# Two-layer decode step: a group's softmax issued ahead of the next group's first K, and the last group's softmax in a place of its own

## The chip, the cores and the metric

The kernel runs on one core of one Trainium2 chip. The metric is the device time of one execution in microseconds (us); a kernel is timed several times and the median is given. Beside the times there is a profile of one execution, taken by the hardware. PE is TensorE's matmul pipe (PEld its weight loads), DVE is VectorE, ACT is ScalarE, POOL is GpSimd, and SP is SyncE, which here does nothing but issue the transfers (DMAs) in a fixed order. SBUF is the on-chip memory, PSUM the place where matmuls leave their results.

## The reference

One token of width 640 passes twice through an attention block and a mixer with an MLP, with the same weights and the same caches both times:

```python
x = x + A(layernorm(x))     # layer 0 in the code, the first layer
x = x + B(layernorm(x))
x = x + A(layernorm(x))     # layer 1 in the code, the second layer
x = x + B(layernorm(x))
```

A has 32 heads of 192 elements, each with its own K and V: `q = x @ wq`, scores of q with the last W = 4096 rows of K, divided by sqrt(192), a softmax `p` over these 4096, `o = p @ V`, and `o @ wo`. B is a layer norm, `gelu(x @ w1)`, a shift along the sequence, `@ w2`, a residual sum, and `gelu(layernorm(x1) @ w3) @ w4`. With one token the four shifts bring only zeros in, so that the path through w1 and w2 gives nothing; the kernel loads w3 and w4 alone. All is bf16. K and V of one head are 1.5 MB each, and they do not fit on the chip: both layers read most of them from HBM, 216 MB in all.

## The kernel before, in words

**Heads and groups.** Heads go in 8 groups of 4 (`QH`), in layer 0 from the last heads to the first (`GROUPS[0].reverse()`): 28 to 31, 24 to 27, and so on, then 8 to 11 (`gi` = 5), 4 to 7 (`gi` = 6) and 0 to 3 (`gi` = 7). Layer 1 goes from the first group to the last. The main loop, from L797, does two things in one turn `gi`: it multiplies the softmax of group `gi` with that group's V, and it makes the scores of group `gi + 1` from that group's K.

**Steps.** Their names in the code and their main lines are:

- `T(h, half)`: two of the four quarters of a head's K are transposed by DVE (L422).
- `S(h, half, ...)`: the scores of these quarters, 12 matmuls into `ST_ps` (L501).
- `softmax_steps` (L521) gives seven steps for a group. `part_max`: maximum per partition (L529, DVE). `turn_max`: its transpose on PE (`pmT_ps`, L535). `full_max`: the maxima per head, written out wide (L544 to L548, DVE). `spread_max`: broadcast by a matmul (`nb_ps`, L557), then the exponentials on ACT (L565). `turn_p`: P's transpose on DVE (L570) and its sums (L572, L573). `swap`: P brought into the order in which V lies (`PT_ps`, L582, on PE; L585 on ACT), and the total `l_ps` (L588). `recip`: its reciprocal (L595, L597, DVE).
- `pv(layer, h, hq, PT, first, mid)`: P V of one head, 16 matmuls into `O_ps` (L629). After every second head DVE transposes `O_ps` into `o_sb` (L638), and `o_fold` (L640) sums up from there by matmuls (`oT_ps`, L649) and scales on ACT (L652). `mid` is a step that is issued in the middle of the 16 matmuls.
- `qproj_steps` (four steps: project, spread, repeat, block): the query of the group after next (L452, L466, L473, L483).
- `out_row` with its sums (L678, L688), `turn_row` (L700), `out_proj` (L660) and `add_y`: the group before goes through wo, and into the residual sum.

In a turn these are interleaved: the first K quarters of the next group come ahead of `part_max`, its other transposes and scores between the further softmax steps, and so on. The two last turns are special: in the last but one (`hurry`), the remaining K heads are transposed and scored after the second P V, and the last group's softmax is made in the same turn around the fourth P V. The last turn (`final`) only multiplies with V.

**Places.** K, V, wo, w3 and w4 live in 11 cells (`cells`) of 1.5 MB. A written plan (`home`, L118) says which cell a load goes to. The loads are issued by SP in one fixed order (`stream`, L283). A load waits until its cell has been read by whatever used it, and all loads behind it in the order wait with it. Around the change the order is, with cells in brackets: K 4 and 5 [0, 1], V 8 and 9 [2, 3], K 6 [4], V 10 [7], K 7 [9], V 11 [8], wo of group 2 [0], K 0 [2], V 4 [7, and a last piece into the small buffer `kx`], K 1 [4], V 5 [10], K 2 [8], K 3 [7], V 6 [0], V 7 [10], V 0 [8], wo, V 1 [0], wo, V 2 [8], V 3 [7], w3 [0], w4 [8]. Cell 10 holds the transposed K of the heads that aren't kept until head 7 has been scored. K of heads 0 to 6 stays on chip, transposed, for layer 1. Parts of w3 and w4 are kept for both layers in `wx_sb`; until they are loaded, rows of that buffer serve as scratch (`row_space`, L397), and in layer 1 `kx` does.

**Order on the engines.** On PE, DVE, ACT and SP each engine executes its instructions in the order in which the code issues them (`manual_schedule`); a wait holds all that stands behind it on the same engine. Small PSUM results share two places (`psm`, `bufs=2`). In the softmax, the wide maxima and P lie in the bytes of `o_sb` (`o_bytes`, L519), so a softmax and an O that is being folded can't be there at once:

```python
    o_sb = big.tile([P, 2, NA, 32], F32, name="o_sb")
    o_bytes = o_sb[:].rearrange("p e c i -> p (e c i)").bitcast(BF16)
```

Of the kernel before, what the change touches and what calls it, by code (L numbers as in the profile page):

```python
# [8 lines left out]
F32 = mybir.dt.float32  # L9
# [7 lines left out]
P = 128  # L17
# [17 lines left out]
def kernel(  # L35
# [482 lines left out]
    o_sb = big.tile([P, 2, NA, 32], F32, name="o_sb")  # L518
    o_bytes = o_sb[:].rearrange("p e c i -> p (e c i)").bitcast(BF16)  # L519

    def softmax_steps(n, ST_ps, sc):  # L521
        held = {}

        def by_head(t):
            return t.rearrange("p (x e) -> p e x", e=2)

        def part_max():
            pm = big.tile([P, 2], F32, name="pm")
            nc.vector.tensor_reduce(out=pm[:], in_=by_head(ST_ps), op=ALU.max, axis=AX.X)  # L529
            held["pm"] = pm  # L530

        def turn_max():
            pmT_ps = psm.tile([1, 2 * (P + HB)], F32, tag="psm")
            for e in range(2):
                nc.tensor.transpose(pmT_ps[0:1, e * P:(e + 1) * P], held["pm"][:, e:e + 1], ident[:, :])  # L535
            held["pmT"] = pmT_ps

        def full_max():
            ngm = big.tile([1, 2, 2], F32, name="ngm")
            wide = o_bytes[0:1, SW:3 * SW].bitcast(F32)  # L540
            own = held["pmT"][0:1, :].rearrange("o (e y) -> o e y", e=2)[:, :, 0:P]
            for e in range(2):
                rows = wide[:, e * P:(e + 1) * P].rearrange("o (q e x) -> o q e x", q=NT, e=2)
                nc.vector.memset(rows[:, :, 1 - e], NEVER)  # L544
                nc.vector.tensor_reduce(  # L545
                    out=ngm[0:1, e], in_=own[:, e].rearrange("o (q x) -> o q x", q=NT)[:, :, 0:HB].rearrange(
                        "o q (r z) -> o r q z", r=2), op=ALU.max, axis=AX.XY, negate=True)
                nc.vector.tensor_scalar(  # L548
                    out=rows[:, :, e].rearrange("o q (r z) -> o q r z", r=2),
                    in0=ngm[0:1, e].unsqueeze(1).unsqueeze(3).broadcast_to([1, NT, 2, 2 * NM]),  # L550
                    scalar1=sc[0:1, 0:1], scalar2=None, op0=ALU.mult)
            held["w"] = wide

        def spread_max():
            nb_ps = psm.tile([P, 2], F32, tag="psm")
            for e in range(2):
                nc.tensor.matmul(nb_ps[:, e:e + 1], lhsT=held["w"][:, e * P:(e + 1) * P],  # L557
                                 rhs=one[0:1, 0:1], start=True, stop=True)
            nb_sb = big.tile([P, 2], F32, name="nb_sb")
            nc.scalar.copy(nb_sb[:], nb_ps[:])  # L560
            Pr = o_bytes[:, 0:SW]
            held["PrT"] = o_bytes[:, SW:2 * SW]
            lpart = big.tile([P, 2], F32, name="lpart")
            for e in range(2):
                nc.scalar.activation(out=by_head(Pr)[:, e], in_=by_head(ST_ps)[:, e], func=ACTF.Exp,  # L565
                                     bias=nb_sb[:, e:e + 1], scale=sc[:, 0:1], accum_out=lpart[:, e:e + 1])
            held["Pr"], held["l"] = Pr, lpart

        def turn_p():
            nc.vector.transpose(held["PrT"], held["Pr"])  # L570
            lh = big.tile([P, QH], F32, name="lh")
            nc.vector.tensor_add(held["l"][:, 0:1], held["l"][:, 0:1], held["l"][:, 1:2])  # L572
            nc.vector.tensor_scalar(out=lh[:], in0=hm[:], scalar1=held["l"][:, 0:1], scalar2=None, op0=ALU.mult)  # L573
            held["lh"] = lh

        def swap():
            ng = NGK // NT
            PT_ps = psm.tile([P, 2 * n, NJ4, NGK], F32, tag="psm")
            src = held["PrT"].rearrange("p (g j i) -> p i j g", g=ng, j=NJ4)
            for m in range(NM):  # L580
                for q in range(NT):
                    nc.tensor.matmul(PT_ps[32 * m:32 * (m + 1), :, :, ng * q:ng * (q + 1)], lhsT=Eq[:, q, :],  # L582
                                     rhs=src[:, m:QW:NM], start=True, stop=True)
            PT = big.tile([P, n, NJ4 * NGK, 2], BF16, name="PT")
            nc.scalar.copy(PT[:].rearrange("p h c e -> p e h c"),  # L585
                           PT_ps[:].rearrange("p (e h) j g -> p e h (j g)", e=2))
            l_ps = psm.tile([P, QH], F32, tag="psm")
            nc.tensor.matmul(l_ps[:], lhsT=ones, rhs=held["lh"][:], start=True, stop=True)  # L588
            held["lps"] = l_ps
            return PT  # L590

        def recip():
            lq = big.tile([P, QH], F32, name="lq")
            rl = sm.tile([P, 1], F32, name="rl")
            nc.vector.scalar_tensor_tensor(out=lq[:], in0=held["lps"][:], scalar=1.0, in1=blkm[:],  # L595
                                           op0=ALU.mult, op1=ALU.mult, accum_out=rl[:, 0:1])
            nc.vector.reciprocal(rl[:], rl[:])  # L597
            return rl

        return part_max, turn_max, full_max, spread_max, turn_p, swap, recip  # L600
# [103 lines left out]
    def attention(layer, x_cur, rs_cur, x_new, z_new, rs_new, ss_new):  # L704
# [13 lines left out]
        def T(h, half):  # L718
            for q in (2 * half, 2 * half + 1):
                if (h, q) not in Th:  # L720
                    Th[h, q] = transpose_quart(layer, h, q)
# [75 lines left out]
        for gi, cur in enumerate(groups):  # L797
            nxt = list(enumerate(groups[gi + 1])) if gi + 1 < len(groups) else []
            ST_n = None
            if nxt:  # L800
# [24 lines left out]
                else:  # L825
                    if gi == 0:
                        for step in q1:
                            step()
                    h0 = nxt[0][1]
                    T(h0, 0)  # L830
                    part_max()
                    T(h0, 1)
                    S(h0, 0, ST_n, 0)
                    turn_max()
                    full_max()
                    S(h0, 1, ST_n, 0)
                    spread_max()
                    h1 = nxt[1][1]
                    q = None
                    if gi + 2 < len(groups):  # L840
                        q = qproj_steps(groups[gi + 2][0] // QH, xc, row=q_row if gi in rows else None)
# [2 lines left out]
                    in_row = gi - 1 in rows  # L844
                    if pending is not None:
                        y_ps = out_row(layer, *pending, acc, gi - 1 == rows[0]) if in_row else out_proj(layer, pending)
                    turn_p()
                    T(h1, 0)
                    if q:
                        q[1]()  # L850
                        q[2]()
                    if in_row:
                        y_ps()
                        if gi - 1 == rows[-1]:
                            add_y(turn_row(acc), 1 if layer == 1 and gi + 2 == len(groups) else 2)
                        pending = None
                    if pending is not None:
                        add_y(y_ps, 1 if layer == 1 and gi + 2 == len(groups) else 2)
                        pending = None
                    PT = swap()  # L860
                    T(h1, 1)
                    if q:
                        q[3]()
                    rl = recip()
                    nxt.pop(0)
            else:
                PT, rl = early
# [6 lines left out]
                order = [order[n] for n in (VC, VP, 0, 1)]  # L874
            for n, (hq, h) in enumerate(order):
                first = n % 2 == 0
                pv(layer, h, hq, PT, first, fold)
                if final:
                    if layer == 0 and hq == 0:
                        add_y(out_proj(layer, pending), 1)  # L880
                    if hq == 1:
                        center_y()
                    fold = None
                    if not first:
                        def fold(h=h):
                            o_fold(h, oT, rl)

                    continue
                if hurry and hq == 1:
                    (q2, h2), (q3, h3) = nxt  # L890
                    for half in range(2):
                        T(h2, half)
                        S(h2, half, ST_n, q2)
                    T(h3, 0)
                    S(h3, 0, ST_n, q3)
                    T(h3, 1)
                elif hurry and hq == 2:
                    S(h3, 1, ST_n, q3)
                    steps = softmax_steps(len(cur), ST_n, sc)
                    steps[0]()  # L900
                    steps[1]()
                elif nxt and not (hurry and hq == 3):
                    q2, h2 = nxt.pop(0)
                    for half in range(2):
                        T(h2, half)
                        S(h2, half, ST_n, q2)
                if not first:
                    o_fold(h, oT, rl, len(groups) - 4 > gi >= 2 * layer)
                if hurry and hq == 3:
                    for step in steps[2:5]:  # L910
                        step()
                    early = steps[5](), steps[6]()
            if final:
                fold()
# [151 lines left out]
```

## Time and profile before

| | |
|---|---|
| median of 3 runs | 522.64 us (521.62 to 523.77) |
| the profiled execution's own time | 522.96 us |
| its span (first to last instruction) | 521.2 us |
| busy: PE, DVE, ACT | 60%, 55%, 9% of the span |
| mean granted TensorE clock | 0.709 of full speed |
| read from HBM | 216.47 MB, 415 GB/s over the span |
| DMA engines, share of the span | 98.1% for SP's queue |

How to read it: the page cuts the span into 40 equal slices of 13 us and gives for each the busy tenths of every engine, the granted clock, the DMA engines' share and GB/s. The chain that ended last is the work followed back from the last instruction, at each step to what released it. A row of the timeline is start, duration, engine, line, operation, destination and source, count, and in brackets the idle time ahead of it on its engine with what ended it. "SPq" is SP's queue, where a row is the issue of a transfer and not its landing.

### The profile page before, as it was taken

How to read it: one execution, taken by the hardware profiler on the slowest of the kernel's cores; microseconds unless marked ns; L12 is line 12 of the kernel's file. 1: busy time of each engine (PE TensorE's matmuls, PEld its weight loads, DVE VectorE, ACT ScalarE, POOL GpSimd, SP SyncE). 2: the span in 40 equal slices, each digit the busy share in tenths (PEclk: the TensorE clock that was granted, in tenths of full speed). 3: DMA queues.
4: the chain of work that ended last, by engine and by line, in shares of the span. 5: the costliest groups of instructions: out<-in, count | busy, mean ns of one | idle time of the engine just before them, and what ended most of it. 6: DMA issues, size and time to landing. Idle time of an engine off the chain costs nothing.

```text
span 521.2 us, 9518 instructions
## 1 busy us (share of the span) xinstructions
PE 314.6 (60%) x4132; PEld 195.0 (37%) x4132; DVE 285.3 (55%) x642; ACT 48.8 (9%) x173; POOL 4.0 (1%) x16
## 2 busy tenths in 40 slices
PE   1045866656473664767655876757485674645776
PEld 0023434324242332545333644433243342333445
DVE  2057576657564674476623366657446674646723
ACT  1000101010010100101011111010010100100011
POOL 2000000000000000000000000000000000000000
PEclk9999568756778566566765687686656677875667
DMA  8999999999999999979999999999999999999995
GB/s 349 436 434 433 418 441 428 429 435 424 440 429 429 429 431 426 427 309 397 429 423 415 371 419 430 433 435 427 428 437 428 430 433 430 425 436 426 423 409 226
DMA packets 17613, 217.07 MB, mean 417 GB/s; under 512 B 1828, under 2 KB 2340, under 8 KB 7972
## 3 DMA queue, kind: packets, MB, share of 16 engines
q1 hardware_dynamic: 17572, 216.48, 98.1%
q8 instruction: 32, 0.52, 0.4%
q14 instruction: 9, 0.07, 0.0%
HBM read 216.47 MB, written 0.00 MB: 415 GB/s over the span
## 4 chain that ended last, share of the span: by engine, by line
DMA 45%; PE 24%; DVE 23%; ACT 4%; issue 3%; SPq 1%; DVEq 0%; ACTq 0%
DMA cells<-in_A_k_cache_dram 40%; DVE cells L422 16%; PE ST_ps L501 10%; PE O_ps L629 4%; DMA cells<-in_A_v_cache_dram 4%; ACT o_sb L565 3%; PE nb_ps L557 2%; DMA cells<-in_B_w_dram 2%; PE pmT_ps L535 1%; PE PT_ps L582 1%; DVE o_sb L570 1%; DVE o_sb L638 1%; DVE pm L529 1%; PE y_ps L700 1%; PE y_ps L1011 1%
## 5 line engine op out<-in xcount | busy, mean ns | idle before, releaser
L422 DVE STREAM_TRANSPOSE cells<-cells 128x768 uint32<-128x768 uint32 x228 | 203.7, 946 | 49.2 <-DMA cells<-in_A_k_cache_dram 49.0
L501 PE MATMUL ST_ps<-cells,Qblk 128*32 128x256 bf16 x1536 | 150.0, 373 | 118.0 <-DVE pm L529 65.7
L501 PEld LDWEIGHTS <-Qblk 128*32 128x32 bf16 x1536 | 89.6, 123 | 174.6 <-issue 154.1
L629 PE MATMUL O_ps<-cells,PT 128*4 128x384 bf16 x1018 | 93.5, 450 | 10.4 <-DMA cells<-in_A_v_cache_dram 10.0
L638 DVE STREAM_TRANSPOSE o_sb<-O_ps 128x384 f32<-128x384 f32 x32 | 18.7, 583 | 78.2 <-PE O_ps L629 78.2
L629 PEld LDWEIGHTS <-PT 128*4 128x4 bf16 x1024 | 43.5, 103 | 26.7 <-issue 16.3
L652 ACT ACTIVATE oT<-oT_ps,rl 64x6 bf16<-64x6 f32 x32 | 8.4, 262 | 228.8 <-PE oT_ps L649 128.3
L570 DVE STREAM_TRANSPOSE o_sb<-o_sb 128x256 bf16<-128x256 bf16 x16 | 7.1, 445 | 37.7 <-ACT o_sb L565 37.7
L582 PE MATMUL PT_ps<-o_sb,Eq 128*32 128x64 bf16 x256 | 11.0, 293 | 10.7 <-DVE lpart L572 5.5
L560 ACT COPY nb_sb<-nb_ps 128x2 f32<-128x2 f32 x16 | 2.6, 161 | 134.8 <-PE nb_ps L557 134.8
L582 PEld LDWEIGHTS <-Eq 128*32 128x32 bf16 x256 | 7.4, 112 | 20.5 <-issue 20.4
L565 ACT ACTIVATE o_sb<-ST_ps,nb_sb,sc 128x128 bf16<-128x128 f32 x32 | 15.0, 491 | 0.5
L452 PE MATMUL qT_ps<-xc,wq_sb 128*128 128x1 bf16 x210 | 7.1, 165 | 13.0 <-DMA wq_sb<-in_A_wq_dram 12.1
L557 PEld LDWEIGHTS nb_ps<-one,o_sb 1*128 1x128 f32 x64 | 12.2, 261 | 6.9 <-issue 4.9
L557 PE MATMUL nb_ps<-one,o_sb 1*128 1x1 f32 x64 | 13.6, 309 | 1.5 <-DVE ngm L545 1.5
L678 PE MATMUL yr_ps<-cells,oT 128*1 128x320 bf16 x108 | 14.5, 432 | 0.0
L441 PE MATMUL qr_ps<-wq_sb,xc 128*1 128x384 bf16 x90 | 13.5, 452 | 0.0
L588 PE MATMUL l_ps<-lh,one 128*128 128x4 f32 x32 | 8.3, 329 | 6.8 <-ACT PT L585 6.8
L466 DVE TENSOR_TENSOR Xq<-qT_ps,maskq 128x24 bf16<-128x24 f32 (+1 forms) x18 | 2.8, 155 | 16.9 <-PE qT_ps L452 16.9
L452 PEld LDWEIGHTS <-wq_sb 128*128 128x128 bf16 x210 | 6.7, 101 | 14.0 <-DMA wq_sb<-in_A_wq_dram 13.2
L649 PE MATMUL oT_ps<-o_sb,Lq 128*32 128x6 f32 x160 | 7.2, 190 | 7.7 <-DVE o_sb L638 7.7
L585 ACT CAST PT<-PT_ps 128x256 bf16<-128x256 f32 x16 | 7.1, 445 | 47.8 <-PE PT_ps L582 47.8
(146 smaller groups left out, 193.9 us busy)
## 6 DMA issues: line engine op xcount, KB each, us to landing
cells<-in_A_k_cache_dram SPq DMA_DIRECT2D x23, 3072.0 KB, 20.5
cells<-in_A_v_cache_dram SPq DMA_DIRECT2D x22, 3072.0 KB, 22.6
cells<-in_A_v_cache_dram SPq DMA_DIRECT2D x12, 1536.0 KB, 12.5
cells<-in_A_k_cache_dram SPq DMA_DIRECT2D x11, 1536.0 KB, 13.7
cells<-in_A_wo_dram SPq DMA_DIRECT2D x13, 960.0 KB, 28.3
wq_sb<-in_A_wq_dram SPq DMA_DIRECT2D x5, 1536.0 KB, 13.7
cells<-in_A_v_cache_dram SPq DMA_DIRECT2D x6, 768.0 KB, 15.2
cells<-in_A_v_cache_dram SPq DMA_DIRECT2D x2, 1248.0 KB, 11.4
```

Source lines behind the costliest of these rows:

```text
L422: nc.vector.transpose(Tu, Ku[:, :, q * NY:(q + 1) * NY])
L441: nc.tensor.matmul(qr_ps[32 * i:32 * i + 1, :], lhsT=xc[:, kc:kc + 1], rhs=wq_sb[:, kc, t0 * P + i * N:t0 * P + (i + 1) * N], start=(kc == ...
L452: nc.tensor.matmul(qT_ps[:, tl:tl + 1], lhsT=wq_sb[:, kc, t * P:(t + 1) * P], rhs=xc[:, kc:kc + 1], start=(kc == 0), stop=(kc == ND - 1))
L501: nc.tensor.matmul(ST_ps[r:r + QW, :].rearrange("p (g i) -> p g i", g=ng), lhsT=Q[:, n, :], rhs=T4[:, :, f, :, t], start=(hq == 0 and n == ...
L557: nc.tensor.matmul(nb_ps[:, e:e + 1], lhsT=held["w"][:, e * P:(e + 1) * P], rhs=one[0:1, 0:1], start=True, stop=True)
L565: nc.scalar.activation(out=by_head(Pr)[:, e], in_=by_head(ST_ps)[:, e], func=ACTF.Exp, bias=nb_sb[:, e:e + 1], scale=sc[:, 0:1], accum_out ...
L570: nc.vector.transpose(held["PrT"], held["Pr"])
L582: nc.tensor.matmul(PT_ps[32 * m:32 * (m + 1), :, :, ng * q:ng * (q + 1)], lhsT=Eq[:, q, :], rhs=src[:, m:QW:NM], start=True, stop=True)
L629: nc.tensor.matmul(O_ps[r:r + 4, :], lhsT=PT[:, hq, 2 * i:2 * i + 2].rearrange("p c e -> p (c e)"), rhs=v_pair(V, h, 2 * i * Dh, 2 * Dh), ...
L638: nc.vector.transpose(o_sb[:], O_ps.rearrange("p (e a c) -> p e c a", e=2, c=NA))
L652: nc.scalar.activation(oT[r, :], oT_ps[r, :], ACTF.Copy, scale=rl[r, 0:1])
L678: nc.tensor.matmul(yr_ps[32 * i:32 * i + 1, :], lhsT=oT[:, k:k + 1], rhs=wo_t[:, k * D + i * N:k * D + (i + 1) * N], start=(k == 0), stop= ...
```

## The change

It has three parts.

First, in layer 0, in the turns `gi` = 5 and 6 (`ahead`), the first four softmax steps of group `gi` are issued before any K of the next group, and `turn_p` before the first transpose of K; the query's steps, the row sums, `swap` and `recip` follow that first transpose, then scores and the other transposes. Both heads `h0` and `h1` are transposed before the first P V. All other turns keep their order.

Second, in the last but one turn of both layers (`hurry`), the scores of the last quarter of K and the maximum (`steps[0]`) are issued ahead of the third head's P V, the next three steps right behind it, and `turn_p` (`steps[4]`) in the middle of the fourth.

Third, that last group's softmax gets a place of its own (`room`): a part of `wx_sb` in layer 0, where w4 is loaded later, and `kx` in layer 1, in place of the bytes of `o_sb`.

```diff
-    def softmax_steps(n, ST_ps, sc):
+    def softmax_steps(n, ST_ps, sc, room=None):
+        room = o_bytes if room is None else room
...
-            wide = o_bytes[0:1, SW:3 * SW].bitcast(F32)
+            wide = room[0:1, SW:3 * SW].bitcast(F32)
...
-            Pr = o_bytes[:, 0:SW]
-            held["PrT"] = o_bytes[:, SW:2 * SW]
+            Pr = room[:, 0:SW]
+            held["PrT"] = room[:, SW:2 * SW]
...
-                    h0 = nxt[0][1]
-                    T(h0, 0)
-                    part_max()
-                    T(h0, 1)
-                    S(h0, 0, ST_n, 0)
-                    turn_max()
-                    full_max()
-                    S(h0, 1, ST_n, 0)
-                    spread_max()
-                    h1 = nxt[1][1]
+                    h0, h1 = nxt[0][1], nxt[1][1]
+                    ahead = layer == 0 and gi + 3 >= len(groups)
+                    if ahead:
+                        for step in (part_max, turn_max, full_max, spread_max):
+                            step()
+                    else:
...
+                    if ahead:
+                        turn_p()
+                        T(h0, 0)
+                        if q:
+                            q[1]()
+                        if in_row:
+                            y_ps()
+                        else:
+                            add_y(y_ps, kind)
+                        PT, rl = swap(), recip()
+                        S(h0, 0, ST_n, 0)
+                        T(h0, 1)
+                        if q:
+                            q[2]()
+                            q[3]()
+                        if in_row and gi - 1 == rows[-1]:
+                            add_y(turn_row(acc), kind)
+                        S(h0, 1, ST_n, 0)
+                        T(h1, 0)
+                        T(h1, 1)
+                    else:
...
-                pv(layer, h, hq, PT, first, fold)
+                if hurry and hq == 2:
+                    S(h3, 1, ST_n, q3)
+                    steps = softmax_steps(len(cur), ST_n, sc, (wx_sb[:, 16 * P:22 * P], kx)[layer])
+                    steps[0]()
+                pv(layer, h, hq, PT, first, steps[4] if hurry and hq == 3 else fold)
...
                 elif hurry and hq == 2:
-                    S(h3, 1, ST_n, q3)
-                    steps = softmax_steps(len(cur), ST_n, sc)
-                    steps[0]()
-                    steps[1]()
+                    for step in steps[1:4]:
+                        step()
...
                 if hurry and hq == 3:
-                    for step in steps[2:5]:
-                        step()
                     early = steps[5](), steps[6]()
```

More of the change, by code (lines that the diff above doesn't have):

```diff
@@ L828, in attention @@
                             step()
-                    h0 = nxt[0][1]
-                    T(h0, 0)
-                    part_max()
-                    T(h0, 1)
-                    S(h0, 0, ST_n, 0)
-                    turn_max()
-                    full_max()
-                    S(h0, 1, ST_n, 0)
-                    spread_max()
-                    h1 = nxt[1][1]
+                    h0, h1 = nxt[0][1], nxt[1][1]
[5 more added lines that the diff above has]
+                        T(h0, 0)
+                        part_max()
+                        T(h0, 1)
+                        S(h0, 0, ST_n, 0)
+                        turn_max()
+                        full_max()
+                        S(h0, 1, ST_n, 0)
+                        spread_max()
                     q = None
@@ L846, in attention @@
                         y_ps = out_row(layer, *pending, acc, gi - 1 == rows[0]) if in_row else out_proj(layer, pending)
[L847 to L864, printed above, removed]
+                    kind = 1 if layer == 1 and gi + 2 == len(groups) else 2
+                    if ahead:
+                        turn_p()
+                        T(h0, 0)
+                        if q:
[5 more added lines that the diff above has]
+                        PT, rl = swap(), recip()
+                        S(h0, 0, ST_n, 0)
+                        T(h0, 1)
+                        if q:
[3 more added lines that the diff above has]
+                            add_y(turn_row(acc), kind)
+                        S(h0, 1, ST_n, 0)
+                        T(h1, 0)
+                        T(h1, 1)
+                    else:
+                        turn_p()
+                        T(h1, 0)
+                        if q:
+                            q[1]()
+                            q[2]()
+                        if in_row:
+                            y_ps()
+                            if gi - 1 == rows[-1]:
+                                add_y(turn_row(acc), kind)
+                        elif pending is not None:
+                            add_y(y_ps, kind)
+                        PT = swap()
+                        T(h1, 1)
+                        if q:
+                            q[3]()
+                        rl = recip()
@@ L865, in attention @@
+                    pending = None
                     nxt.pop(0)
```

## The prediction

> **What bounds the kernel now.** I read the page's slices and chain first, then the busy time of stretches, then the issues of SP's queue, then the instructions between them. The page:
>
> ```profile
> DMA  8999999999999999979999999999999999999995
> GB/s 349 436 434 433 418 441 428 429 435 424 440 429 429 429 431 426 427 309 397 429 423 415 371 419 430 433 435 427 428 437 428 430 433 430 425 436 426 423 409 226
> ...
> DMA cells<-in_A_k_cache_dram 40%; DVE cells L422 16%; PE ST_ps L501 10%; PE O_ps L629 4%; DMA cells<-in_A_v_cache_dram 4%; ACT o_sb L565 3%; PE nb_ps L557 2%; DMA cells<-in_B_w_dram 2%; PE pmT_ps L535 1%; PE PT_ps L582 1%; DVE o_sb L570 1%; DVE o_sb L638 1%; DVE pm L529 1%; PE y_ps L700 1%; PE y_ps L1011 1%
> ```
>
> The DMA engines move some 430 GB/s in nearly every slice, and K's transfers are 40% of the chain that ends last: a stream of bytes sets the time. Beside start and end, three slices fall short: the 18th (309 GB/s) with the 19th (397), and the 23rd (371), the border of the two layers. What can be won is what the stream loses there. The first dip, by stretches: the stretch, its length, busy us of PE, PEld, DVE, ACT and POOL with their instructions, the granted TensorE clock, the DMA engines' busy share, GB/s:
>
> ```profile
> 206.00:209.00 3.00, 3.00 (x25) 1.39 (x21) 2.19 (x8) 0.00 (x0) 0.00 (x0) 0.50 0.91 389
> 209.00:212.00 3.00, 3.00 (x44) 2.30 (x46) 0.75 (x4) 1.15 (x5) 0.00 (x0) 0.50 1.04 442
> 224.00:227.00 3.00, 1.57 (x13) 0.90 (x13) 3.00 (x5) 0.00 (x0) 0.00 (x0) 0.50 1.01 430
> 227.00:228.00 1.00, 0.72 (x13) 0.39 (x12) 1.00 (x2) 0.00 (x0) 0.00 (x0) 0.50 0.81 344
> 228.00:231.00 3.00, 2.92 (x48) 2.07 (x46) 2.92 (x4) 0.26 (x1) 0.00 (x0) 0.50 0.25 107
> 231.00:233.00 2.00, 1.67 (x27) 1.10 (x26) 0.29 (x1) 0.00 (x0) 0.00 (x0) 0.89 0.78 205
> 233.00:242.00 9.00, 5.54 (x84) 3.66 (x84) 5.70 (x15) 1.74 (x7) 0.00 (x0) 0.79 1.00 375
> 242.00:290.00 48.00, 29.82 (x444) 18.72 (x444) 21.49 (x64) 4.73 (x20) 0.00 (x0) 0.61 1.02 422
> 302.00:514.00 212.00, 134.59 (x1753) 83.75 (x1752) 121.35 (x263) 20.80 (x75) 0.71 (x2) 0.70 1.01 428
> 498.00:501.00 3.00, 1.44 (x26) 0.63 (x27) 1.46 (x7) 0.26 (x1) 0.00 (x0) 1.00 1.01 412
> ```
>
> A full queue gives 422 to 428 GB/s; I count with 425. Against that, 227 to 228 lacks 81 KB, 228 to 231 lacks 3 x 318 = 954 and 231 to 233 2 x 220 = 440: 1475 KB, or 1475 / 425 = 3.5 us of stream lost. 233 to 242, where the engines are busy again but slow, lacks 9 x 50 = 450 KB, another 1.1 us. Why the queue ran dry stands among SP's issues (start, duration) and in what SP waited for:
>
> ```profile
> 198.47 0.60 SPq L164 DMA_DIRECT2D cells<-in_A_k_cache_dram  x1
> 212.55 0.54 SPq L178 DMA_DIRECT2D cells<-in_A_v_cache_dram  x1
> ...
> 220.48 0.53 SPq L164 DMA_DIRECT2D cells<-in_A_k_cache_dram  x1
> 229.96 0.54 SPq L178 DMA_DIRECT2D cells<-in_A_v_cache_dram  x1
> ```
> ```profile
> SPq L178 <- PE O_ps L629: 8.9, 1, 8.9
> ```
>
> The load at 229.96 is V of head 4. Its place is cell 7, which V of head 10 holds until the product P V of that head (L629) has read it, and SP, which issues in order, stood 8.9 us for it. So the length of the work from K of heads 4 and 5 (landed at 203.39) to P V of head 10 (229.96) decides: 26.6 us. The instructions of that stretch:
>
> ```profile
> 197.90 0.58 DVE L638 STREAM_TRANSPOSE o_sb<-O_ps 128x384 f32<-128x384 f32 x1 [3.01 <-PE O_ps L629]
> ...
> 198.53 0.30 PE L649 MATMUL oT_ps<-o_sb,Lq 128*32 128x6 f32 x8 [0.68 <-DVE o_sb L638]
> ...
> 203.39 1.84 DVE L422 STREAM_TRANSPOSE cells<-cells 128x768 uint32<-128x768 uint32 x2 [4.91 <-DMA cells<-in_A_k_cache_dram]
> 205.15 0.39 DVE L529 TENSOR_REDUCE pm<-ST_ps 128x2 f32<-128x256 f32 x1
> ...
> 205.59 1.47 PE L501 MATMUL ST_ps<-cells,Qblk 128*32 128x256 bf16 x12 [6.75 <-DVE pm L529]
> ...
> 213.69 0.96 DVE L688 TENSOR_TENSOR wx_sb<-wx_sb,yr_ps 1x320 f32<-1x320 f32 x2
> ...
> 214.71 2.26 PE L700 MATMUL y_ps<-ident,wx_sb 33*128 33x1 f32 x12 [0.71 <-DVE wx_sb L688]
> ...
> 218.47 0.59 PE L588 MATMUL l_ps<-lh,one 128*128 128x4 f32 x2 [0.59 <-ACT PT L585]
> 218.99 1.45 PE L629 MATMUL O_ps<-cells,PT 128*4 128x384 bf16 x16
> 219.30 0.16 DVE L597 RECIPROCAL rl<-rl 128x1 f32<-128x1 f32 x1
> ...
> 223.45 0.58 DVE L638 STREAM_TRANSPOSE o_sb<-O_ps 128x384 f32<-128x384 f32 x1 [3.99 <-PE O_ps L629]
> ...
> 236.77 0.59 PE L535 MATMUL pmT_ps<-ident,pm 128*1 128x128 f32 x2
> ...
> 240.43 0.45 DVE L570 STREAM_TRANSPOSE o_sb<-o_sb 128x256 bf16<-128x256 bf16 x1 [2.12 <-ACT o_sb L565]
> ```
>
> DVE idles 4.91 us ahead of 203.39, for K. The scores of heads 8 to 11 are complete by then, but their softmax starts only at 205.15, interleaved with the new K, so P V of head 8 begins at 218.99.
>
> **Part 1: the softmax ahead (layer 0, groups of heads 8 to 11 and 4 to 7).** No operation is added; they move. DVE is free from 197.90 + 0.58 = 198.5. The maximum is 0.39; from its turn (236.77) to P's transpose (240.43) took 3.66, and the transpose is 0.45, with two small sums behind it at the 0.16 of the row of 219.30: 198.5 + 0.4 + 3.7 + 0.8 = 203.4. That fits the idle 4.91 us almost exactly, so K's transpose starts at 203.4 as before. Then, in the new order:
>
> - K of head 4, first half, 1.84: 205.2. Behind it on DVE stand a step of the query (0.16) and the row sums, 0.96: 206.4. The turn of P on PE runs beside them; it waits only for the query's step, which gives a PSUM place back.
> - The row total l_ps 0.59 and the reciprocal, 2 x 0.16: 207.4. Second half of K, 1.84: 209.3; the first half's scores (1.47) lie beside it.
> - The turned row y_ps, 2.26 on PE, from about 209.0, with its sum: 211.5. Then the second scores, 1.47: 212.8. Both halves of head 5's transposes, 2 x 1.84 behind that sum: 215.2.
> - P V of head 8, 1.45 beside the transposes: 214.3. Head 5's scores need the last transpose: 215.2 + 1.47 = 216.7. P V of head 9: 216.7 + 1.45 = 218.1.
>
> O's transpose (L638) thus starts at about 218.1, against 223.45: 5.3 us earlier. From there the order is the old one, so V of head 4 is issued near 229.96 - 5.3 = 224.7; the K ahead of it follows P V of head 8, near 214.3 instead of 220.48. V of head 8 should not hold this up: its 3 MB were queued right behind K of heads 4 and 5, so they land near 203.4 + 3.146 MB / 425 GB/s = 210.8 (an estimate from these rows).
>
> When must the issue come? The engines were full until 227, and the issue of 229.96 brought bytes only in the row of 231: about 1.1 us. So 226 keeps them full; 224.7 leaves 1.3 us. The next loads in SP's order wait for transposes and P V that move with it.
>
> For the next group, heads 4 to 7, the same softmax (0.4 + 3.7 + 0.8 = 4.9 us) stands between O's transpose, 5.3 us earlier, and the transposes of K of head 0. These start no later than now, with the softmax already behind them, so the loads that this group's P V releases come early enough for a stream that is ahead by 3.5. The **gain is 3.5 us** if the queue no longer dries up; I take that, because it is the part with idle engines. The bounds: 2.9 by the busy share alone (0.19 + 3 x 0.75 + 2 x 0.22 = 2.9), and 4.5 if the slow 233 to 242 was all restart too. I leave that 1.1 us out, because V of head 4 is cut in two pieces in the new order too.
>
> **Part 2: the last maximum ahead, P in its own place.** In layer 0 it is covered by transfers: the chain there runs through landings (K 10.81 and B_w 8.53, below). In layer 1 nothing covers it:
>
> ```profile
> 231.24 10.81 DMA cells<-in_A_k_cache_dram
> ...
> 279.44 8.53 DMA cells<-in_B_w_dram
> ...
> 450.04 19.11 DMA cells<-in_A_k_cache_dram
> 469.24 1.84 DVE cells L422 x2
> ```
> ```profile
> 497.90 0.42 DVE L529 TENSOR_REDUCE pm<-ST_ps 128x2 f32<-128x256 f32 x1 [2.38 <-PE ST_ps L501]
> ...
> 498.69 0.82 PE L629 MATMUL O_ps<-cells,PT 128*4 128x384 bf16 x16
> ...
> 503.74 0.70 PE L582 MATMUL PT_ps<-o_sb,Eq 128*32 128x64 bf16 x16 [1.80 <-DVE lpart L572]
> ...
> 504.98 1.45 PE L629 MATMUL O_ps<-cells,PT 128*4 128x384 bf16 x16
> ```
>
> From 469.24 to the end the chain is work alone. Before: maximum 497.90, turn of P 503.74, last group's P V 504.98. After: the scores no longer wait for the third P V, so the maximum comes some 0.85 earlier, 497.05. Its turn now stands behind that P V on PE (497.0 + 1.45): 498.5. 3.66 later, 502.1, P's transpose, with its sums to 502.9; O's transpose is queued behind it on DVE, 0.58: 503.5; the fold's matmuls, 0.30 and a start just behind it (198.53 after 198.48): 503.9; there the turn of P may start. So 0.2 later than now, where the fourth P V had no wait ahead of it. With the third P V at 0.82 in place of 1.45 it is 0.5 earlier; with 0.4 more lost in the 3.66 to a slower clock (its pmT alone is 0.59), 0.6 later than now. I take **0**, with -0.5 to +0.6. The fresh place costs no copy; it only frees this softmax from waiting until O has been read.
>
> A rule bears on those bounds. The Trainium skill (TensorE: Matmul & The Clock Gate, Part 1) has TensorE's clock halved by default and released after some 3.4 us of sustained work; the new wait inside the fourth P V's queue would by that rule cost the 0.4 and so the 0.6, and 522.64 would become 519.7 rather than 519.1. The trace does not follow the rule here: 1.00 was granted in 498 to 501 with PE busy under half the time, and 0.50 through 206 to 212 with PE busy throughout.
>
> **Sum.** The profiled execution took 522.96 us for a span of 521.2; with 3.5 less it is 519.5. The median of the three runs is 0.32 below that execution: 522.64 - 3.5 = **519.1 us**. A stretch gained before 242 is kept if the queue stays full (422 and 428 GB/s in the two long rows) and the border's dip, which starts from a landing (279.44, 8.53), shifts with it.
>
> **Rivals.** (B) The queue still dries up, for less time. For it: only 1.3 us of margin, and a softmax that fits its gap to 0.1 us. Against it: the rows are those of the half-speed clock already. Each us beyond the margin costs a us; with 2 to 3 us too late about 1.3 us is won: 521.3. (C) The transfer is hidden anyway: what the first layer wins is given back at the border (371 GB/s in the 23rd slice would sink further), or the tail is the real bound. For it: the tail from 469.24 has no transfer in its chain. Against it: that chain starts at a landing. It gives 522.6, with the tail's -0.5 to +0.6. (D) Slower: on PE the scores of head 4 now stand behind the turn of P and l_ps, which stand behind DVE's rows, which stand behind K's transpose. If these waits follow one another rather than overlap, the stretch from 203.39 to head 10 grows. It decides once it is longer than the present 26.6 us (my sum: 21.3); at 29.6 the queue is dry for 3 us more, and the time is 525.6. Against it: it takes 5.3 us of error in ten short rows.
>
> **How the numbers follow.** A measurement of this kernel tells about 0.5%, 2.6 us, from no change. Forecast 0.60 (517.5 to 519.9), B 0.17, C 0.12, D 0.11. The low end is 522.64 - 4.5 - 0.5 = 517.6; the high end reaches over B to C's middle, 522.6. Left out are D, half of C and a little below: under 0.2. Faster by over 0.5%: the forecast but for its slow edge, 0.58; within: 0.02 + 0.17 + 0.12 = 0.31; slower: 0.11.
>
> **What would show it.** In the changed profile: the softmax between 198.5 and 203.4; P V of head 8 near 213 to 214 rather than 218.99; V of head 4 issued before 226; no stretch under 0.9 DMA share between 224 and 242; the border's landing (287.97 now) and the last K's (469.15 now) both some 3.5 us earlier; the last group's first P V as far behind the last K as now (504.98 - 469.2 = 35.8 us, to within 0.6). I am wrong if V of head 4 is issued after 227, or if the last K lands earlier and the end doesn't follow.

## The result and the profile after

The changed kernel takes 519.02 us (median of 6, 518.16 to 519.44) against 523.20 us of the kernel before, measured beside it: a ratio of 0.992, 95% interval 0.9901 to 0.9939. The profiled execution took 518.16 us with a span of 516.4, against 522.96 and 521.2.

The stretches of the profile after, in the same columns as before (last three: granted clock, DMA share, GB/s):

```profile
224.00:227.00 3.00, 2.16 (x35) 1.16 (x28) 1.39 (x3) 0.00 (x0) 0.00 (x0) 1.00 1.01 423
227.00:228.00 1.00, 0.46 (x10) 0.33 (x10) 0.76 (x3) 0.20 (x1) 0.00 (x0) 1.00 0.99 419
228.00:231.00 3.00, 1.86 (x36) 1.59 (x35) 0.90 (x6) 1.21 (x6) 0.00 (x0) 0.74 0.99 413
231.00:233.00 2.00, 0.99 (x18) 0.68 (x17) 1.97 (x5) 0.44 (x1) 0.00 (x0) 0.50 1.01 426
233.00:242.00 9.00, 6.59 (x55) 3.68 (x56) 5.83 (x11) 0.00 (x0) 0.00 (x0) 0.50 1.02 432
```

The dry stretch is gone. From 227 to 242 the rows now carry 419 + 3 x 413 + 2 x 426 + 9 x 432 = 6398 KB; before they carried 344 + 3 x 107 + 2 x 205 + 9 x 375 = 4450. At 425 GB/s the difference is 4.6 us, and the span is 4.8 us shorter. The slow 233 to 242 went with the rest. V of head 4 still comes in two pieces, and the rows from 227 to 233, in which most of their packets move, hold 413 to 426 GB/s. The packet records of the two traces show the difference: the 128 packets of the larger piece, 9984 bytes each, all took 375 ns in the full queue, where they had averaged 499 behind the gap.

The instructions that made the room (timeline after; lines behind L521 are one higher than before, later ones more):

```profile
197.87 0.39 DVE L530 TENSOR_REDUCE pm<-ST_ps 128x2 f32<-128x256 f32 x1
...
201.48 0.45 DVE L571 STREAM_TRANSPOSE o_sb<-o_sb 128x256 bf16<-128x256 bf16 x1 [1.74 <-ACT o_sb L566]
...
203.38 1.84 DVE L422 STREAM_TRANSPOSE cells<-cells 128x768 uint32<-128x768 uint32 x2 [1.16 <-DMA cells<-in_A_k_cache_dram]
...
216.49 0.58 DVE L639 STREAM_TRANSPOSE o_sb<-O_ps 128x384 f32<-128x384 f32 x1 [2.29 <-PE O_ps L630]
```

The softmax of heads 8 to 11 lies wholly in the wait for K, which still ends at 203.4; of the 4.91 us of idle DVE 1.16 are left. O's transpose after the second P V comes at 216.49 instead of 223.45. SP's queue shows what follows:

```profile
213.25 0.54 SPq L164 DMA_DIRECT2D cells<-in_A_k_cache_dram  x1
222.90 0.54 SPq L178 DMA_DIRECT2D cells<-in_A_v_cache_dram  x1
```

V of head 4 is issued at 222.90 instead of 229.96, and K of head 0 at 213.25 instead of 220.48. At the other end, the chain of work in order of time (start, length) and what PE waited for in the last 10 us:

```profile
444.87 19.43 DMA cells<-in_A_k_cache_dram
...
502.01 10.45 DMA cells<-in_B_w_dram
```
```profile
PE V_ps L990 <- DMA cells<-in_B_w_dram: 0.6, 1, 0.6
...
PE y_ps L1037 <- DMA cells<-in_B_w_dram: 0.2, 1, 0.2
```

The last K lands at 464.3 instead of 469.15, 4.85 us earlier: what was won at 240 is carried through the border and the whole second layer. At the end, the last products of the MLP now wait for the last pieces of w3 and w4. Before, the profile shows no such wait behind the last K, yet there too the work had nothing to spare. The last input bytes come at 517.3 before and at 512.5 after (by the packet records), both times 3.9 us ahead of the end of the span. The stretches there, two of before and two of after:

```profile
517.00:517.40 0.40, 0.40 (x20) 0.40 (x18) 0.10 (x1) 0.00 (x0) 0.00 (x0) 0.50 0.05 19
517.40:518.00 0.60, 0.60 (x26) 0.60 (x24) 0.00 (x0) 0.00 (x0) 0.00 (x0) 0.50 0.00 0
```
```profile
512.00:512.60 0.60, 0.42 (x16) 0.34 (x14) 0.02 (x1) 0.00 (x0) 0.00 (x0) 0.50 0.06 21
512.60:513.20 0.60, 0.60 (x25) 0.60 (x25) 0.00 (x0) 0.00 (x0) 0.00 (x0) 0.50 0.00 0
```

### The profile page after: what moved, and what is told of

The parts are those of the page before. It is cut to its first block, busy times and chain, and to the rows that moved or that the text cites. A ratio compares the mean times of both kernels' runs of the same rounds, so it can differ in the third digit from the quotient of the medians.

```text
span 516.4 us, 9514 instructions
## 1 busy us (share of the span) xinstructions
PE 318.0 (62%) x4132; PEld 197.3 (38%) x4132; DVE 285.2 (55%) x642; ACT 48.6 (9%) x173; POOL 4.0 (1%) x16
## 5 line engine op out<-in xcount | busy, mean ns | idle before, releaser
L501 PE MATMUL ST_ps<-cells,Qblk 128*32 128x256 bf16 x1536 | 157.6, 381 | 108.2 <-DVE cells L422 52.9
L501 PEld LDWEIGHTS <-Qblk 128*32 128x32 bf16 x1536 | 92.2, 125 | 166.9 <-issue 145.6
L630 PE MATMUL O_ps<-cells,PT 128*4 128x384 bf16 x1018 | 96.8, 447 | 9.5 <-DMA cells<-in_A_v_cache_dram 9.2
L630 PEld LDWEIGHTS <-PT 128*4 128x4 bf16 x1024 | 45.4, 102 | 24.9 <-issue 14.1
L583 PE MATMUL PT_ps<-o_sb,Eq 128*32 128x64 bf16 x224 | 9.6, 292 | 10.1 <-DVE Xq L466 3.4
L558 PEld LDWEIGHTS nb_ps<-one,o_sb 1*128 1x128 f32 x56 | 10.4, 252 | 7.4 <-issue 4.3
L566 ACT ACTIVATE o_sb<-ST_ps,nb_sb,sc 128x128 bf16<-128x128 f32 x28 | 13.1, 491 | 0.5
L558 PE MATMUL nb_ps<-one,o_sb 1*128 1x1 f32 x56 | 11.7, 302 | 2.0 <-DVE ngm L546 2.0
L679 PE MATMUL yr_ps<-cells,oT 128*1 128x320 bf16 x108 | 12.9, 394 | 0.0
L650 PEld LDWEIGHTS oT_ps<-o_sb,Lq 128*32 128x32 f32 x160 | 6.1, 131 | 14.8 <-DVE o_sb L639 14.1
```

Source lines behind the costliest of these rows:

```text
L501: nc.tensor.matmul(ST_ps[r:r + QW, :].rearrange("p (g i) -> p g i", g=ng), lhsT=Q[:, n, :], rhs=T4[:, :, f, :, t], start=(hq == 0 and n == ...
L630: nc.tensor.matmul(O_ps[r:r + 4, :], lhsT=PT[:, hq, 2 * i:2 * i + 2].rearrange("p c e -> p (c e)"), rhs=v_pair(V, h, 2 * i * Dh, 2 * Dh), ...
L650: nc.tensor.matmul(oT_ps[r0 + 32 * n:r0 + 32 * (n + 1), :], lhsT=Lq[:], rhs=o, start=(e == 0), stop=(e == len(terms) - 1))
L679: nc.tensor.matmul(yr_ps[32 * i:32 * i + 1, :], lhsT=oT[:, k:k + 1], rhs=wo_t[:, k * D + i * N:k * D + (i + 1) * N], start=(k == 0), stop= ...
```

## The experiments

Two theories were in play after the result. A: the whole gain is that V of head 4 is issued before the queue runs dry. B: the tail, where the trace seemed to show 1.3 to 1.6 us less work behind the last K, has a part in it. Two more, C and E, are put in words by the expectations in which they first stand; these letters are not those of the prediction's rivals. Eight kernels were run, all against the kernel before; the expectations below were written before the runs.

**The parts one by one.** The first kernel keeps the softmax ahead and puts the last group's softmax back:

```diff
-                if hurry and hq == 2:
-                    S(h3, 1, ST_n, q3)
-                    steps = softmax_steps(len(cur), ST_n, sc, (wx_sb[:, 16 * P:22 * P], kx)[layer])
-                    steps[0]()
-                pv(layer, h, hq, PT, first, steps[4] if hurry and hq == 3 else fold)
+                pv(layer, h, hq, PT, first, fold)
...
```

> The softmax ahead in the last steps of layer 0, the last group's softmax as before (in the bytes of o_sb, fourth P V ahead of its maxima). Theory A (all of the gain is the stretch in which the queue was dry; the end is held by the last bytes, so the shorter tail of the whole change buys nothing): V of head 4 issued at 222.9, no stretch under 0.9 DMA share between 224 and 242, and 518.8 to 519.4 us, as the whole change. Theory B (the tail's 1.3 to 1.6 us, which the trace of the whole change shows on the engines, are part of its gain): 520.3 to 520.6.

Measured: 518.61 us, ratio 0.9927 (0.9914 to 0.994), and V of head 4 issued at 222.92. This is theory A; the whole change is not faster than this half of it.

The second has only the other half (`ahead = False`):

> Only the last group's softmax in its new order and place, in both layers; all turns ahead of it as before. The dry stretch of 227 to 233 stays. Theory A: the tail's chain gets shorter by 1.3 to 1.6, but the last transfer ends at 516.3 and the work behind it takes 3.9, so no more than about 1.0 can be won: 522.2 to 523.2. Theory B: all of it counts, 521.6 to 521.9.

Measured: 522.48 us, ratio 0.9997 (0.9988 to 1.0006). The dry stretch is there (228 to 231 at 115 GB/s, V of head 4 issued at 229.86), and no gain can be told. The 516.3 of the expectation is where the last group of matmuls starts in the trace of before, not where the last transfer ends; that is 517.3, so there was nothing to win at all, and not 1.0.

The third and fourth split the first half by turns (`gi + 3 == len(groups)` and `gi + 2 == len(groups)`):

> The whole change, but the softmax goes ahead in the turn of heads 8 to 11 alone; in the turn of heads 4 to 7 the old order. Theory A (what matters is when V of head 4 can be issued): V of head 4 at 222.9 and 519.0 to 519.6. Theory C (the queue needs both turns, or it dries up one turn later, near 240 to 250): 520.5 to 522.

Measured: 520.64 us, ratio 0.9965 (0.9953 to 0.9977). Theory A in its narrow form falls here: V of head 4 was issued at 222.38, and still 1.6 to 2 us of the gain were missing. Its stretches show where:

```profile
239.00:242.00 3.00, 1.90 (x30) 1.22 (x33) 2.93 (x7) 0.45 (x1) 0.00 (x0) 0.50 0.99 422
242.00:245.00 3.00, 3.00 (x48) 2.24 (x43) 1.53 (x5) 0.00 (x0) 0.00 (x0) 0.50 0.74 264
245.00:248.00 3.00, 1.35 (x10) 0.39 (x4) 1.89 (x3) 0.00 (x0) 0.00 (x0) 0.84 0.93 359
```

The queue runs almost dry one turn later. The next load that waits for a P V is K of head 3, in the cell of V of head 4; SP stood for it as it had stood for V of head 4:

```profile
SPq L164 <- PE O_ps L630: 8.6, 1, 8.6
```

Its issue in the kernel before, in this one and in the whole change:

```profile
244.16 0.54 SPq L164 DMA_DIRECT2D cells<-in_A_k_cache_dram  x1
242.79 0.54 SPq L164 DMA_DIRECT2D cells<-in_A_k_cache_dram  x1
237.99 0.54 SPq L164 DMA_DIRECT2D cells<-in_A_k_cache_dram  x1
```

With the softmax ahead in that turn too, the dip is gone: 242 to 245 and 245 to 248 hold 433 and 430 GB/s.

> The whole change, but the softmax goes ahead in the turn of heads 4 to 7 alone. V of head 4 is issued at about 230 as before and the dry stretch stays. Theory A: 522.2 to 523.2, as with the last group's part alone. Theory C: this turn has a share of its own, 520.5 to 522.

Measured: 522.51 us, ratio 0.9999 (0.999 to 1.0008), V of head 4 at 229.66. The second turn alone buys nothing, since the stream has already stopped at the first.

**The dose.** If the issue of V of head 4 is the cause, moving it back must bring the loss back. Three kernels repeat one transpose of K of head 6 on the stretch ahead of P V of head 10; nothing else changes:

```diff
-        nc.vector.transpose(Tu, Ku[:, :, q * NY:(q + 1) * NY])
+        for _ in range(4 if (layer, h, q) == (0, 6, 3) else 1):
+            nc.vector.transpose(Tu, Ku[:, :, q * NY:(q + 1) * NY])
```

> The whole change, with the last quarter of K of head 6 transposed three times more than needed (same values, same place): 3 x 0.87 = 2.6 us of DVE work more on the stretch ahead of P V of head 10. Theory A (the queue must get V of head 4 by about 226.4, ahead of that nothing counts): its issue goes from 222.9 to 225.5, within the margin, and the time stays at 518.6 to 519.4. Theory E (the work on that stretch counts by itself, us by us): 521.5.

> The same with six transposes more, 5.2 us. Theory A: V of head 4 issued at 228.1, 1.7 us past the margin, a dry stretch of that length comes back and the time is 520.7 to 522. Theory E: 524.1. If the margin is wider than thought: 519.

> The same with ten transposes more, 8.7 us. Theory A: V of head 4 issued at 231.6, 5.2 us past the margin, later than in the kernel before, so slower than that or equal to it: 524 to 525.5. Theory E: 527.6.

| kernel | V of head 4 issued | median us | ratio to before, interval |
|---|---|---|---|
| whole change | 222.90 | 519.02 | 0.992 (0.9901 to 0.9939) |
| softmax ahead in both layers (the last experiment below, same chip as the delays) | 222.30 | 518.65 | 0.9932 (0.9918 to 0.9945) |
| three transposes more | 225.81 | 519.80 | 0.9956 (0.9939 to 0.9973) |
| six more | 228.88 | 521.68 | 0.9989 (0.998 to 0.9999) |
| before | 229.96 | 522.07 to 523.20 | 1 |
| ten more | 232.05 | 525.56 | 1.0065 (1.0048 to 1.0082) |

The time follows the issue, over the whole range and past the kernel before. The three loads ahead of it (V of head 11, wo, K of head 0), which the change also issues earlier, don't explain this: in the delayed kernels they are issued within 1 us of the whole change (at 201.7 to 202.9, 208.6 to 208.8 and 212.9 to 213.1). The sizes were 2.9, 6.0 and 9.2 us of delay where 2.6, 5.2 and 8.7 were counted. Against the kernel of the last experiment, which shared their chip, six transposes more cost 3.0 us, not 5.2, so theory E is out. But the sharp margin of theory A is out as well: counted from 222.30 the first 3.5 us of delay cost 1.2, the next 3.1 cost 1.9, and the last 3.2 cost 3.9. With three transposes more, the issue at 225.81 was ahead of the margin of 226.4, and yet the two rows from 227 to 233 lack 462 KB against 425 GB/s, or 1.1 us:

```profile
227.00:230.00 3.00, 2.45 (x27) 1.43 (x23) 0.52 (x2) 0.00 (x0) 0.00 (x0) 0.63 0.96 378
230.00:233.00 3.00, 2.11 (x44) 1.70 (x44) 1.29 (x8) 0.85 (x4) 0.00 (x0) 0.94 0.94 318
```

The engines are called busy 94 to 96% of the time and move 318 to 378 GB/s. With ten more the same stands behind a real gap:

```profile
230.00:233.00 3.00, 2.97 (x47) 2.11 (x43) 3.00 (x4) 0.26 (x1) 0.00 (x0) 0.50 0.01 4
233.00:236.00 3.00, 2.27 (x35) 1.53 (x34) 0.90 (x4) 0.00 (x0) 0.00 (x0) 0.80 0.89 246
236.00:239.00 3.00, 2.18 (x39) 1.83 (x37) 0.91 (x6) 1.08 (x5) 0.00 (x0) 0.77 0.97 281
```

**The end.** The last kernel takes the softmax of the last group but one out of the tail, by the same order in layer 1, in the two turns ahead of the last (`ahead = gi + 3 >= len(groups)`):

> The whole change, and the softmax ahead in the same two turns of layer 1 as well, which shortens the work behind the last K by taking 3 to 4 us of softmax out of it. Theory A (the end is held by the last bytes of wo, w3 and w4): 518.4 to 519.4, as the whole change. Theory B (the tail is a chain of work from the last K): 515.5 to 517.

Measured: 518.65 us, ratio 0.9932 (0.9918 to 0.9945). The first P V of the last group came at 493.85 instead of 498.52, 4.7 us earlier, and the time did not move. What PE waited for from there on:

```profile
PE O_ps L630 <- DMA cells<-in_A_v_cache_dram: 2.3, 3, 1.4
...
PE y_ps L661 <- DMA cells<-in_A_wo_dram: 1.1, 3, 0.6
PE V_ps L990 <- DMA cells<-in_B_w_dram: 0.9, 1, 0.9
```

The tail's head start is given back to V, wo and w3 on the way. The end is held by the last bytes: in all ten traces they come 3.8 to 4.1 us ahead of the end of the span. This kernel and the one with only the softmax ahead are no slower than the whole change, and not faster by more than the runs of one kernel differ; the fewest edits with the whole gain are those of the latter.

## Why the prediction was right, and where it wasn't

**The bound and the mechanism: right.** A stream of bytes sets the time, and the change moves the one issue on which the stream had stopped. The dose shows it, in both directions.

**The stretch: right, with a softer sum.** P V of head 10 releases its cell at 222.9; 224.7 was counted. The softmax, with its sums, took 197.87 to 202.23, 4.4 us, where 4.9 was counted, and the fit to 0.1 us that the prediction named as a risk was a gap of 1.16 us. The step that waits for the turned row ended sooner too: O's transpose came at 216.49, and 218.1 was counted.

**The gain's size: within its bounds, the wrong part left out.** 3.5 was taken and 4.5 named as the upper bound, leaving out 1.1 us for the slow stretch from 233 to 242, on the ground that V of head 4 comes in two pieces. In a full queue their packets take 375 ns in place of 499: the slowness was the restart, and all 4.6 us went. By medians the gain is 4.2, by the profiled executions 4.8, a little above the bound. That the forecast of 519.1 meets 519.02 to 0.1 us is luck: the gain is 0.7 larger than forecast, and the kernel before, measured again beside the changed one, took 523.20 in place of 522.64.

**The second turn: named, but not counted.** The prediction concluded that its loads come early enough, since they start "no later than now" with the softmax behind them. The conclusion held; the reason is too weak. A stream that is ahead by over 4 us meets the next wait for a P V earlier, K of head 3 in the cell of V of head 4. With the old order there this load was issued at 242.79, 1.4 us earlier than in the kernel before, and 1.6 to 2 us of the gain were still lost (520.64). The softmax ahead in that turn as well is what keeps the first turn's gain, and no sum of the prediction shows by how much it had to be earlier.

**The margin: not a point.** "226 keeps them full" was too simple. The rate sinks before the queue is empty, and the cost grows with the delay rather than from a point on. I read that as a queue with too little in it; its depth was not measured.

**The tail: 0, and 0 it was, though its sum did not decide.** The trace after seemed to contradict the sum, with 34.1 us from K's transpose to the last group's first P V where the kernel before had 35.7 and no change was forecast. The granted clock goes with the difference. Where it was 1.00 during the third P V, the old order has 498.43 - 464.72 = 33.7 us (the kernel with the softmax ahead alone) and the new one 33.4 to 33.9 (heads 4 to 7 alone, three and ten transposes more): no change, as forecast. Where it was 0.50, the old order has the 35.7 of before; where it was 0.60 to 0.63, the new one has 34.1 to 34.4 (the whole change and three others). No pair of the two orders has the same slow clock, so what the order gives there stays open. It does not matter for the time, since emptying the tail by 4.7 us changed nothing. There the prediction overlooked something: it read the tail as work alone, with no transfer in its chain, but the last input bytes came 3.9 us ahead of the end in that trace too, so a shorter tail had nothing to win.

**The rule on the clock.** The Trainium skill (TensorE: Matmul & The Clock Gate, Part 1) has sustained work release the clock and idleness halve it. The trace after does not agree, as that of before did not: 1.00 was granted in 224 to 227 with PE busy 2.16 of 3 us, and 0.50 in 233 to 242 with PE busy 6.6 of 9.

**The rivals of the prediction.** B (the queue still dries up, for less time) is near to what the kernel with only the first turn ahead shows, though there the queue runs almost dry one turn later: 520.6, where 521.3 was written. D's price was 525.6 for 3 us more. Ten transposes took 525.56, but with an issue only 2.1 us later than before. That is 3.5 us over the median of the kernel before beside it (522.07), and 2.3 by the profiled executions (525.24 and 522.96), so the equal figure is luck. C did not come: the border loses about what it lost before, 24 x (425 - 386) = 0.94 MB in 278 to 302 before and 27 x (425 - 392) = 0.89 MB in 272 to 299 after.

## What to carry to other kernels

In a kernel that a stream of transfers sets, look for the slices where the rate falls, find the one issue that the queue stood for, and shorten the work that releases its place; then look one turn further, for a stream that comes earlier meets the next wait earlier. Work that depends on nothing new, like a softmax whose scores are complete, belongs into the wait for data rather than behind it. A stretch gained inside such a stream is kept to the end, but a shorter tail is worth nothing where the last bytes are late.

## What the runs showed of the hardware

A queue that has run dry costs more than its dry time. With an issue 2.1 us later than in the kernel before, the six us behind the gap moved 246 and 281 GB/s at a busy share of 0.89 and 0.97; the rows in which the same transfers move in a queue that stays full hold 413 to 426. By the packet records the same packets of 9984 bytes took 375 ns each in the full queue and 523 on average behind this gap. It is not a matter of V's two pieces: where the queue ran almost dry ahead of an uncut K (softmax ahead in the turn of heads 8 to 11 alone), its packets of 12288 bytes took 460 ns each ahead of the dip (238 to 242) and 554 on average from 244 to 248. So a busy share near 1 is no sign of full speed; GB/s is. The Trainium skill (DMA: Bandwidth & Descriptors, Bandwidth, measured) gives a single transfer of 1 MB 341 GB/s and one of 16 MB 425, for transfers issued from GpSimd. These runs, issued from SyncE, agree in kind and not in number: V of head 4, 1.5 MB in two pieces, moved at 246 to 281 just behind a gap, less than the page's 341 for 1 MB; a queue that stays full gave 413 to 432. How much of it is the depth of the queue was not tried by itself.
